# Attention over memories with a spatially gated layer behind it: new written orders for head, steady batches and last batch

## The chip, the cores and the metric

The kernel runs on one core of one Trainium2 chip. Its time is what the device takes for one execution, in microseconds (us). The kernel before took 421.38 us, the median of 3 runs (420.0 to 421.89). One more execution of it was profiled and took 421.2 us.

A core has a matrix engine (TensorE, PE in the profile), three engines for elementwise work (VectorE, DVE; ScalarE, ACT; GpSimd, POOL) and a queue that starts transfers (SyncE, SP). Each works through its own list of instructions in order and waits on semaphores for the others.

## The reference

There are 8 batches of 8 heads with 576 rows of 64 numbers. Each head compresses its keys and values into 32 memories, by weights that are a softmax over the rows; the queries attend to these. The result, 576 rows of 512 numbers, goes through a layer of two halves u and v: v is normalised per row, mixed over the rows by a 576 x 576 matrix, gates u, and is projected.

```python
a = exp(phi - max(phi, axis=rows)); a = a / (sum(a, axis=rows) + 1e-9)
k_m, v_m = einsum("bhsm,bhsd->bhmd", a, k), einsum("bhsm,bhsd->bhmd", a, v)
attn = softmax(q @ k_m.T / sqrt(64));  x = concat_heads(attn @ v_m)
h = maximum(x @ w_in, 0);  u, v = h[..., :512], h[..., 512:]
v_n = (v - mean(v)) / sqrt(var(v) + 1e-6)
out = (u * (w_spatial @ v_n + b_spatial)) @ w_out
```

w_in and w_out arrive as 64-bit floats.

## The kernel before, in words

All work is cut into threads, Python generators that emit a few instructions and stop. One token of a written list is one step of one thread. The letter names the thread, the number its slice (of rows for V and O, of channels for U and G), each quote mark one batch further ahead, and `*n` repeats it. `step` (line 796) starts or advances the thread.

- P (`memory_weights`, 290): loads phi, takes the maximum over rows, transposes it (mt, L300) and back (mb, L309), subtracts (L311), exponentiates (L318), sums (es).
- K (`memories`, 323): loads k and v, two steps of products kvm (L337) and sums, then den, two copies kmn (L364), vmn, transposes tk and tv, copies kT and vT.
- Q (`queries`, 393): loads q and brings it into shape; S (`scores`, 507): products sc (L518), four VectorE transposes (L529), maximum, subtraction, exponential, sum, and the parts ah and al of the result.
- M (`products`, 571): v_m times a half of w_in, mp (L584), rounded to a high part mh on ScalarE and a low part ml. 16 matmuls for each of M0 and M1. The prediction calls them memory products.
- V (`gate`, 598): the v half for 128 rows, pv, six matmuls (L616); V4 is the last 64 rows (L625, L626). Then relu (L621), or for V4 a copy, an addition and a relu (L635 to L637); statistics on VectorE (L640, L642); three small GpSimd steps (L645, L646, L650) that make scale and shift; normalisation on ScalarE (L655); high part vh on ScalarE (L658) and low part vl on VectorE (L660), or for V4 the tiles t1, t2 (L664 to L668).
- U (`units`, 671): the u half for 128 channels, pu (L682), two halves of six matmuls, and a ScalarE copy u (L691).
- G (`spatial`, 696): the mix over rows, ps (L720), in groups of six matmuls: the first reads V0's vh and vl, the second V1's, the third V2's, the fourth V3's and then t1 and t2. Then the gating g on VectorE (L731) and the parts gh, gl (L742, L744).
- O (`project`, 747): po (L760), two steps of six matmuls, a ScalarE copy o (L766) and a transfer out. O4 serves two batches, so it occurs in every second one, and sends two transfers (L771, L772).
- D, E, L, X, W, T, B: loading and decoding w_in and w_out (E and L one half of w_in each; L182 to L190), and preparing the spatial weights (transposes wt, L250). Z: a matmul on a constant tile (L780).

The list START emits the head: batch 0, and the parts of batches 1 and 2 that run ahead. PLAN is then gone through for batches 1 to 7. The order of tokens is the order of instructions on each engine; nothing reorders it later. Which step falls on which pass follows from a count:

```python
for at in sorted(range(len(steps)), key=lambda at: -steps[at][2]):
    key = steps[at][:2]
    upto[at] = count[key] = count.get(key, 0) + 1
...
while b + ahead < B and done.get(key, 0) < upto[at]:
    step(*key)
```

So a step that would lie past batch 7 drops out, and batch 7 goes through what is left of the same list.

The results of TensorE lie in two sets of buffers: four of one bank (tag b1: sc, mp, pv, po, kvm and all transposes) and two of two banks (tag b2: pu, ps, wt). A new tile takes a buffer that the last reader of another has left, so TensorE waits where that reader is late.

In the list before, U3's first half is preceded by V3 and V2, the memory products by U1's second half and four spatial groups after the scores, and in the last batch the copies end with O4 while O0's transfer stands behind O4's. In the head V4 and V3 are multiplied behind batch 1's scores, and on SP batch 1's k and v stand between the second and third of D0's four transfers.

Of the kernel before, what the change touches and what calls it, by code (L numbers as in the profile page):

```python
# [23 lines left out]


START = """
    Q*9 P Q P*2 K P*4 Z P*2 K P D1 P D1 P D1 P Z P Z P Q K*3 D1 P' W K D0 E0 Z K Z K E0 E1 D0 K*2 Z
    E1 K P' S E0 P' E1 S Z K K' P' B T0*2 E0 S P'*2 S*2 K' P' T0 P' S*2 T0 T2 P' S T2 E1 P' S L0 P'
    M1 T3 T2 M1 P' S M1 Z T3 S M1 S M1 T3 S T2 D0 S*2 M1 L0 M1 S P' S P' T3 D0 S*2 P' S*2 T4 S K'
    L1*2 K' L0 V2 V0 Q' K' L1 K'*2 L0 L1 K' V2 V0 T4 T1 B V2 T4*2 M0 V1 M0 Q' P'' T1 M0 X0 V0 T1 S  # L30
    M0 V0 M0 K' X0 U1 T1 V2 X1 Q' K' Q' V1 Q' M0 Q' V1 X1 K'*2 M0 V2 U3 P'' U3 U1 S' U3 P'' K'' S'
    V0 P'' U2 V2 U1 V0 P'' U0 V4 V1*2 V0 S' U0 V3 V1 V2 V4 X0 U2 S'*3 P'' V3 P'' X1 V4*2 M0' U2 U0
    M1' V3 V1 V4*2 X0 V3 X1 V4 V3 S' V3 G0 G1*3 G0 V3 X0 V4 G0 X1 X0 M0' X0 G1*2 G0 M1' G0 M0' X1 X0
    G3 M0' X1 G3 G2 M0' G1 G3 G2 X1 G0 M1' M0' P'' G0 G2 G1 M0' M1' G2 Q'' G3 P'' G0 O0 K'' P'' M1'
    G1 O3 G0 S' G2 G1 G3 G2*2 O1 G3*2 S' O3 S'*2 O3 O0 S' O0 S' P''*2 O3 O2 S' P'' O0 P''*2 S' O1
    M1' S' G2 O1 G3 O2 S' O2 M1' S' G2 O2 S' G3 O1
"""

PLAN = """
    K' V1 V4 U2 V0*2 Q' K'*2 V1*2 U0 V0 K' U2*2 V0 V3 V2 V1 U0 V3 Q' U3*2 U1 V4 V0 K' V2 V3 S' V4*2  # L40
    U3 U1 V2 S' G0*2 S'*2 V2 U1 V2*2 V3 S' G1*2 V3 V4 P'' V3 M1' S' M0' V2 M0' V4 G1 M1' S' V4 V3 S'
    M0'*2 G0 G1*2 G0 G3*2 P'' M0' G3 G0*3 G2 P'' G1 S' G0 G1 G2 P'' G0 G1 G2*2 P'' M1'*2 S' G2 G1 G3
    P'' M0' M1' O3 M1' G2 G3 M0' G2 G3*2 Q'' S' G3 O1 S' P'' Q'' M1' P'' O1 O3 G2 O2 S' O1 O3 P'' O2
    S' P'' S' P'' S' G2 S'*2 K''*2 O0 G3 S' O3 O2 O0 K'' O1 O0 V1' O2 V0' Q'' K'' Q'' V1' O4*2 P'''
    V0' K''' P''' K''' O4 V4' O4 U0' V1' P''' O0 K'' P'''
"""

ON_VECTOR = set("wtl1 wtl4 ml110 ml111 ml100 ml101 E0 E1 L0 L1 X0.sign X1.sign X0 X1".split())
# [2 lines left out]
def memory_attention_spatial_gate(  # L51
# [30 lines left out]
    B, H, S, D = q.shape  # L82
# [3 lines left out]
    P = 128  # L86
# [707 lines left out]
    threads, done = {}, {}  # L794

    def step(kind, n, b):
        key = kind, n, b
        if key not in threads:
            threads[key] = (WEIGHTS if kind in WEIGHTS else BATCH)[kind](b, n)
        done[key] = done.get(key, 0) + 1  # L800
        next(threads[key], None)

    def tokens(plan):
        for kind, n, ahead, times in re.findall(r"([A-Z])(\d?)('*)(?:\*(\d+))?", plan):
            for _ in range(int(times or 1)):
                yield kind, int(n or 0), len(ahead)

    steps = list(tokens(PLAN))  # L810
    upto, count = {}, {}
    for at in sorted(range(len(steps)), key=lambda at: -steps[at][2]):
        key = steps[at][:2]
        upto[at] = count[key] = count.get(key, 0) + 1

    E = mybir.EngineType
    with tc.manual_schedule(engines={E.PE, E.DVE, E.Activation, E.Pool, E.SP}):
        for kind, n, ahead in tokens(START):
            step(kind, n, ahead)
        for b in range(1, B):  # L820
            for at, (kind, n, ahead) in enumerate(steps):
                key = kind, n, b + ahead
                while b + ahead < B and done.get(key, 0) < upto[at]:
                    step(*key)


# [28 lines left out]
```

## Time and profile before

| | us |
|---|---|
| median of 3 runs | 421.38 |
| the profiled execution | 421.2 |
| its span, first to last instruction | 419.4 |
| TensorE busy | 400.1 (95%) |
| VectorE, ScalarE, GpSimd busy | 287.7, 231.2, 54.0 |
| first matmul | 6.32 |
| end of the last matmul's result copy | 414.71 |

Times in the views count from the span's first instruction. Matmuls are pipelined and their ends are modelled, so the distance from one start to the next tells more than a duration. A bracket behind a row gives how long its engine was idle before it, and what ended that. PEld is the loading of weights into TensorE, which runs beside the matmuls. [...]

### The profile page before, as it was taken

To read this page: it belongs to the slowest core of one execution; us is meant where nothing else is said; L and a number is where in the kernel's file an instruction comes from. 1 tells how busy PE (TensorE), PEld (TensorE's weight loads), DVE (VectorE), ACT (ScalarE), POOL (GpSimd) and SP (SyncE) were. 2 spreads that over 40 slices of the span, in tenths; PEclk is the share of its full clock that TensorE was granted. 3 is DMA by queue.
4 is the path that set the end of the run, shared out by engine and by line. 5 is a ranking of instruction groups with operands and counts; after the bars stand their busy time and mean duration, and the time that the engine had idled before them with its cause. 6 is when DMAs were issued, how large, how long until landed. Compare 5 with 4: busy or idle time off the path is not lost.

```text
span 419.4 us, 9447 instructions
## 1 busy us (share of the span) xinstructions
PE 400.1 (95%) x3965; PEld 337.8 (81%) x3965; DVE 287.7 (69%) x540; ACT 231.2 (55%) x425; POOL 54.0 (13%) x131
## 2 busy tenths in 40 slices
PE   3879998999999999999999999999999999999994
PEld 3446767989797888988798888988798888889983
DVE  1579987986978376977779476967779276844430
ACT  3569887556834376437734476337724476248321
POOL 1000233002300140003200140003200140014000
PEclk9988999999999999999999999999999999999998
DMA  8999990035941992048801991049701100020012
GB/s 295 382 368 244 290 247 37 2 112 111 175 158 58 314 120 35 0 163 260 76 2 59 324 122 18 2 163 264 71 2 76 42 13 0 2 100 2 0 52 75
DMA packets 85790, 50.70 MB, mean 121 GB/s; under 512 B 66226, under 2 KB 70322, under 8 KB 85748
## 3 DMA queue, kind: packets, MB, share of 16 engines
q1 hardware_dynamic: 85748, 50.10, 46.9%
q8 instruction: 31, 0.51, 0.5%
q14 instruction: 11, 0.09, 0.1%
HBM read 40.65 MB, written 9.44 MB: 119 GB/s over the span
## 4 chain that ended last, share of the span: by engine, by line
PE 74%; DVE 7%; ACT 6%; DMA 4%; POOL 4%; issue 2%; SPq 0%; DVEq 0%; POOLq 0%; ACTq 0%
PE ps L720 26%; PE po L760 21%; PE pu L682 7%; PE pv L616 6%; PE mp L584 4%; PE kvm L337 3%; DMA w_rem<-in_moe_w_spatial_dram 2%; PE sc L518 2%; ACT vr L655 2%; POOL sh L650 2%; DVE st L640 1%; POOL rs L646 1%; DMA q_all<-in_q_dram 1%; DMA phi_sb<-in_phi_dram 1%; DVE vr L636 1%
## 5 line engine op out<-in xcount | busy, mean ns | idle before, releaser
L720 PE MATMUL ps<-wth,vh 128*128 128x288 f32 x256 | 56.8, 303 | 1.9 <-ACT vh L658 1.5
L720 PE MATMUL ps<-wth,vl 128*128 128x288 f32 x256 | 55.0, 296 | 0.1
L720 PE MATMUL ps<-wtl,vh 128*128 128x288 f32 x256 | 54.9, 296 | 0.0
L760 PE MATMUL po<-woh,gh 128*128 128x512 f32 x128 | 51.0, 398 | 0.0
L760 PE MATMUL po<-wol,gh 128*128 128x512 f32 x128 | 50.3, 393 | 0.0
L760 PE MATMUL po<-woh,gl 128*128 128x512 f32 x128 | 50.1, 392 | 0.0
L742 ACT CAST gh<-g 128x512 fp32r<-128x512 f32 x32 | 19.1, 620 | 56.0 <-DVE g L731 56.0
L645 POOL TENSOR_SCALAR rs<-mv 128x1 f32<-128x1 f32 (+1 forms) x40 | 10.7, 267 | 286.4 <-DVE mv L642 252.2
L720 PEld LDWEIGHTS ps<-wth,vh 128*128 128x128 f32 x256 | 40.8, 188 | 8.3 <-issue 4.2
L766 ACT COPY o<-po 128x512 f32<-128x512 f32 x36 | 21.1, 586 | 47.7 <-PE po L760 46.9
L720 PEld LDWEIGHTS ps<-wth,vl 128*128 128x128 f32 x256 | 41.2, 188 | 0.5 <-DVE vl L660 0.5
L720 PEld LDWEIGHTS ps<-wtl,vh 128*128 128x128 f32 x256 | 41.3, 188 | 0.0
L731 DVE TENSOR_TENSOR g<-u,ps 128x576 f32<-128x576 f32 x32 | 24.1, 753 | 24.4 <-PE ps L720 24.4
L655 ACT ACTIVATE vr<-vr,sh,rs 128x512 f32<-128x512 f32 (+1 forms) x40 | 32.5, 812 | 10.4 <-POOL sh L650 10.4
L640 DVE BATCH_NORM_STATS2 st<-vr 128x6 f32<-128x512 f32 (+1 forms) x40 | 27.0, 674 | 10.8 <-ACT vr L621 10.8
L660 DVE TENSOR_TENSOR vl<-vr,vh 128x512 fp32r<-128x512 f32 x32 | 22.0, 687 | 17.0 <-ACT vh L658 16.7
L682 PE MATMUL pu<-ah,mh 128*128 128x288 f32 x128 | 29.3, 310 | 0.9 <-ACT u L691 0.8
L760 PEld LDWEIGHTS po<-woh,gl 128*128 128x128 f32 x128 | 24.1, 188 | 5.5
L760 PEld LDWEIGHTS po<-woh,gh 128*128 128x128 f32 x128 | 24.0, 188 | 5.0
L760 PEld LDWEIGHTS po<-wol,gh 128*128 128x128 f32 x128 | 24.1, 188 | 4.7
L682 PE MATMUL pu<-ah,ml 128*128 128x288 f32 x128 | 27.4, 296 | 0.0
L682 PE MATMUL pu<-al,mh 128*128 128x288 f32 x128 | 27.3, 294 | 0.0
(141 smaller groups left out, 853.4 us busy)
## 6 DMA issues: line engine op xcount, KB each, us to landing
kv_sb<-in_k_dram SPq DMA_DIRECT2D x8, 1152.0 KB, 7.7
kv_sb<-in_v_dram SPq DMA_DIRECT2D x8, 1152.0 KB, 9.8
out_dram<-o SPq DMA_DIRECT2D x32, 256.0 KB, 2.2
q_sb<-in_q_dram SPq DMA_DIRECT2D x28, 288.0 KB, 6.2
phi_sb<-in_phi_dram SPq DMA_DIRECT2D x8, 576.0 KB, 4.9
raw<-in_moe_w_in_dram SPq DMA_DIRECT2D x8, 512.0 KB, 11.8
raw<-in_moe_w_out_dram SPq DMA_DIRECT2D x4, 512.0 KB, 7.0
q_all<-in_q_dram SPq DMA_DIRECT2D x1, 1152.0 KB, 5.5
```

The lines of the kernel that those rows point to most:

```text
L337: nc.tensor.matmul(kvm[r][32 * j : 32 * j + 32], phi_sb[halves[r], j, i, :], kv_sb[halves[r], j, :, i * D : (i + 1) * D], start=(i == 0), ...
L584: nc.tensor.matmul(mps[r][32 * j : 32 * j + 32, :], vT[D * r : D * r + D, 32 * j : 32 * j + 32], win_sb[D * r : D * r + D, j, cs], start=True,
L616: nc.tensor.matmul(pv, x[:, r, cs], m[:, r, DM:DFF], start=(n == 0), stop=(n == 5))
L640: nc.vector.bn_stats(st6, vr)
L655: nc.scalar.activation(vr, vr, AF.Identity, bias=sh, scale=rs)
L660: nc.vector.tensor_tensor(vl[:, st, :], vr, vh[:, st, :].bitcast(F32), op=ALU.subtract)
L682: nc.tensor.matmul(pu[:, hf, 0:HALF], m[:, r, cs], a[:, r, hf * HALF : (hf + 1) * HALF], start=(n == 0), stop=(n == 5),)
L720: nc.tensor.matmul(ps[:, hf, 0:HALF], a, w[:, hf * HALF : (hf + 1) * HALF], start=(n == 0), stop=(n == len(ops) - 1),)
L731: nc.vector.tensor_tensor(g.rearrange("p (a s) -> p a s", a=2), u[:, dt, :].rearrange("p (a s) -> p a s", a=2), ps[:, :, 0:HALF], op=ALU.mult,
L742: nc.scalar.copy(hi, x)
L760: nc.tensor.matmul(po, a, w, start=(n == 0), stop=(n == 11))
L766: nc.scalar.copy(o, po)
```

## The change

The lists START and PLAN are written anew, with the same tokens in another order, and a third list, LAST, is added. PLAN now serves batches 1 to 6. Batch 7 follows LAST, in which every token is one step of that batch. The counting moves into a function `written` and is otherwise the same. No operation, tile or buffer count changes.

On the engines the places that the prediction speaks of become these. Steady batch, TensorE: ..., O2, U0 first half of the next batch, V2, U0 second half, U3 first half, tk, tv, U3 second half, V3, U1, scores, one group of G0, M1, M0, G1. ScalarE from O2's copy on: o, kmn, V1's vh, kmn, U2's copy; and after the scores: U1's copy, V4's and V2's normalisation, V4's t1, U3's copy. Head, TensorE: V3 ahead of batch 1's scores; after V4: U3, mt, U3, U0, M0, M1, two groups of G1, one of G0, one of G1, one of G0, then G1's fourth. Head, SP: all four transfers of D0, then k and v. Last batch: O2, O3, O0, O4, O1, and the transfers in that order.

```diff
 START = """
-    Q*9 P Q P*2 K P*4 Z P*2 K P D1 P D1 P D1 P Z P Z P Q K*3 D1 P' W K D0 E0 Z K Z K E0 E1 D0 K*2 Z
-    E1 K P' S E0 P' E1 S Z K K' P' B T0*2 E0 S P'*2 S*2 K' P' T0 P' S*2 T0 T2 P' S T2 E1 P' S L0 P'
-    M1 T3 T2 M1 P' S M1 Z T3 S M1 S M1 T3 S T2 D0 S*2 M1 L0 M1 S P' S P' T3 D0 S*2 P' S*2 T4 S K'
-    L1*2 K' L0 V2 V0 Q' K' L1 K'*2 L0 L1 K' V2 V0 T4 T1 B V2 T4*2 M0 V1 M0 Q' P'' T1 M0 X0 V0 T1 S
-    M0 V0 M0 K' X0 U1 T1 V2 X1 Q' K' Q' V1 Q' M0 Q' V1 X1 K'*2 M0 V2 U3 P'' U3 U1 S' U3 P'' K'' S'
-    V0 P'' U2 V2 U1 V0 P'' U0 V4 V1*2 V0 S' U0 V3 V1 V2 V4 X0 U2 S'*3 P'' V3 P'' X1 V4*2 M0' U2 U0
-    M1' V3 V1 V4*2 X0 V3 X1 V4 V3 S' V3 G0 G1*3 G0 V3 X0 V4 G0 X1 X0 M0' X0 G1*2 G0 M1' G0 M0' X1 X0
-    G3 M0' X1 G3 G2 M0' G1 G3 G2 X1 G0 M1' M0' P'' G0 G2 G1 M0' M1' G2 Q'' G3 P'' G0 O0 K'' P'' M1'
-    G1 O3 G0 S' G2 G1 G3 G2*2 O1 G3*2 S' O3 S'*2 O3 O0 S' O0 S' P''*2 O3 O2 S' P'' O0 P''*2 S' O1
-    M1' S' G2 O1 G3 O2 S' O2 M1' S' G2 O2 S' G3 O1
+    Q Z Q*3 Z P Q P*4 K Q P Q*2 P*2 K P Z P*6 K D1*2 K Z E0 K*3 D1 K Q*2 K D1 E1 E0 E1 P' Z K*2 W D0
+    P' S D0 Q S P' K Z E1 S T2 P' S E0 D0 T0 T2 Z S*3 T2 T0 S T0 D0 E0 T2 L0 E1 S*2 M1 T1 P' S T0 P'
+    S B P' M1*2 T3 L1 S K' P' M1 L0 M1 K' S*2 P'*2 S T3 S M1 T3 S Q' S Q' S P' Z L1 S M1 K' S L0 L1
+    V0 T1 P' L0 V2 V0 V2 L1 T3 T1 V0 P' V0 M0 B M0 P'*2 V0 V2 K' T1 M0*2 T4 K' P'' V0 K'*2 V0 T4 U2
+    Q' M0 K' Q' V2 V1 Q' V2 T4 X1 M0 V3 K' T4 V1 U1 V3 M0 K'*2 V1 S Q' P'' K' V3 V2 X1 U2 S' U2 P''
+    S' U1 X1 P'' V2 P'' S' V1*2 V3 U1 X1 U0 V4 V1 V4 U3 P''*2 S' U3 U0 M0' U3 S' X0 V4 X0 U0 S' M1'
+    V1 V3 G1 S' V4 X0 K'' V3 V4*2 M0' X1 P'' X0 V3 V4 M1' G1 V4 X1 G0 G1 M0'*2 G0 G1 G0 X0 S' G0 M0'
+    G1 Q'' M0' X0*2 K'' G0 X1 S' G3 X0 P''*2 G3 G0 X1 G1 G0*2 M1' G2*2 G1 M0' M1' G3 G2 G0 G3 G2 G1
+    M1' G1 O1 G2 G3 G2*3 M1' G3 P'' O0 G3 S'*2 O3 S' O3 S' O1 O3 S' O1 M1' O3 S'*4 P'' G3 O1 S' O2
+    P'' G2 G3 O2 O0 P''*2 O2 O0 O2 O0
 """
 PLAN = """
-    K' V1 V4 U2 V0*2 Q' K'*2 V1*2 U0 V0 K' U2*2 V0 V3 V2 V1 U0 V3 Q' U3*2 U1 V4 V0 K' V2 V3 S' V4*2
-    U3 U1 V2 S' G0*2 S'*2 V2 U1 V2*2 V3 S' G1*2 V3 V4 P'' V3 M1' S' M0' V2 M0' V4 G1 M1' S' V4 V3 S'
-    M0'*2 G0 G1*2 G0 G3*2 P'' M0' G3 G0*3 G2 P'' G1 S' G0 G1 G2 P'' G0 G1 G2*2 P'' M1'*2 S' G2 G1 G3
-    P'' M0' M1' O3 M1' G2 G3 M0' G2 G3*2 Q'' S' G3 O1 S' P'' Q'' M1' P'' O1 O3 G2 O2 S' O1 O3 P'' O2
-    S' P'' S' P'' S' G2 S'*2 K''*2 O0 G3 S' O3 O2 O0 K'' O1 O0 V1' O2 V0' Q'' K'' Q'' V1' O4*2 P'''
-    V0' K''' P''' K''' O4 V4' O4 U0' V1' P''' O0 K'' P'''
+    V1 K' V1 V0 U2 V4 K' U0 U3 K' V0 Q'*2 V0 V2 Q' V0 U0 K' U3 V3 Q' V2 V3*2 V2 U1 K' U1 K' U1 S'*4
+    V4 V2 V4 S' U3 V2 S' P'' V3 G0 V3*2 M1' V4 M0' G1 G0 V4 V2 P'' G1 V3 M1'*2 S' P'' G1 G0 M1' G0*2
+    Q'' G1 G3*2 S'*2 M0' G0 M0' G1 S' G3 S' M1' P'' M0' G3 S' G2 S' G1 P'' M0' G2*2 P'' G2 G1 P''
+    G0*2 M0' G0 M0' G1*2 O0 G2*2 G3 M1' G3 O3 M1' S' G2 G3 S' P'' O0 S' O3 G2 P''*2 O1 S' O0 P'' S'
+    P''*2 O1 K''*2 S' O3*2 U2' O0 V1' P''' O1 V0' Q'' G3 V1' V0' V1' O1 U2' G3 K'' V4' G2 O4 V1' O4
+    V4' O2 O4 V1' O2 K''' O2 O4 V0' K'' O2 U0' V4' P''' K''' V2'
+"""
+LAST = """
+    U2 V0*4 V1*2 V4*3 U0*2 V2*3 U3*3 V3*4 U1*3 G1*2 V2*2 V3*2 V2 V4 G0*3 V4 G1 V3 G0*2 G1*2 G0*3 G1
+    G0 G2*9 G1 G3*9 O2*4 O3*4 G1 O0*4 G1 O4*4 O1*4
 """
...
-        for b in range(1, B):
-            for at, (kind, n, ahead) in enumerate(steps):
+        for b in range(1, B - 1):
+            for (kind, n, ahead), upto in each:
                 key = kind, n, b + ahead
-                while b + ahead < B and done.get(key, 0) < upto[at]:
+                while b + ahead < B and done.get(key, 0) < upto:
                     step(*key)
+        for kind, n, _ in tokens(LAST):
+            step(kind, n, B - 1)
```

## Rows read from the trace of the kernel before

**Rows 1.** Stretches: us, busy time by engine, TensorE's granted clock, transfers' share, GB/s.
```profile
26.40:28.20 1.80, 0.07 (x2) 0.06 (x2) 0.00 (x0) 1.37 (x2) 0.00 (x0) 0.87 1.03 391
28.20:34.60 6.40, 6.40 (x30) 2.98 (x30) 5.91 (x8) 4.67 (x7) 0.00 (x0) 0.50 1.05 395
...
187.10:232.60 45.50, 45.38 (x467) 39.10 (x466) 34.43 (x67) 25.06 (x48) 6.09 (x15) 1.00 0.50 112
```

**Rows 2.** Chain that ended last, in batch 4: start us, us, what.
```profile
232.59 2.73 PE pv L616 x12
...
244.65 0.67 ACT u L691
245.36 2.65 PE pu L682 x18
248.01 1.13 PE sc L518 x32
...
250.13 3.20 PE ps L720 x24
253.33 1.88 PE mp L584 x32
```

**Rows 3.** TensorE in order of time, batch 2: start us, us, instruction.
```profile
151.12 0.39 PE L616 MATMUL pv<-mh,al 128*128 128x512 f32 x1
151.66 0.53 PE L682 MATMUL pu<-ah,mh 128*128 128x288 f32 x2 [0.16 <-ACT u L691]
```

**Rows 4.** Waits: us in total, times, longest.
```profile
ACT vr L655 <- POOL sh L650: 10.4, 13, 1.4
...
PEld pu L682 <- ACT u L691: 3.3, 6, 0.8
...
PE ps L720 <- DVE t L668: 0.2, 1, 0.2
```

**Rows 5.** TensorE in order of time, end of the head.
```profile
55.94 0.39 PE L626 MATMUL pv<-ml,ah 128*64 128x512 f32 x1
...
61.64 0.53 PE L720 MATMUL ps<-wth,vh 128*128 128x288 f32 x2 [0.37 <-ACT u L691]
...
68.21 0.54 PE L720 MATMUL ps<-wth,vh 128*128 128x288 f32 x2 [1.51 <-ACT vh L658]
```

**Rows 6.** GpSimd in order of time, head.
```profile
49.56 0.27 POOL L650 TENSOR_SCALAR sh<-mv,rs 128x1 f32<-128x1 f32 x1
...
62.01 1.50 POOL L650 TENSOR_SCALAR sh<-mv,rs 64x1 f32<-64x1 f32 x1
```

**Rows 7.** VectorE in order of time, at the same place.
```profile
62.24 2.35 DVE L184 SCALAR_TENSOR_TENSOR raw<-raw 128x1024 int32<-128x1024 int32 x2
```

**Rows 8.** TensorE in order of time, before 40 us.
```profile
28.17 0.45 PE L300 MATMUL mt<-ident,mx 128*128 128x128 f32 x1 [1.73 <-issue]
...
30.58 2.80 PE L584 MATMUL mp<-win_sb,vT 64*32 64x512 f32 x16
...
38.80 2.25 PE L337 MATMUL kvm<-kv_sb,phi_sb 64*32 64x128 f32 x144
```

**Rows 9.** SP's transfers in order of time, end: start us, us to issue.
```profile
414.73 0.47 SPq L771 DMA_DIRECT2D out_dram<-o  x1
...
415.89 0.58 SPq L769 DMA_DIRECT2D out_dram<-o  x1
```

**Rows 10.** ScalarE in order of time, batch 3.
```profile
201.92 0.65 ACT L691 ACTIVATE u<-pu 128x576 f32<-128x576 f32 x1 [1.45 <-PE pu L682]
202.47 0.81 ACT L655 ACTIVATE vr<-vr,sh,rs 128x512 f32<-128x512 f32 x1
```

**Rows 11.** SP's transfers in order of time, head.
```profile
21.71 0.38 SPq L325 DMA_DIRECT2D kv_sb<-in_v_dram  x1
25.39 1.60 SPq L173 DMA_DIRECT2D raw<-in_moe_w_in_dram  x2
```

**Rows 12.** Transfers of line 325 (k and v): issue to landing.
```profile
DMA to landing us min/median/max: 6.8/9.1/13.4
```

More of the change, by code (lines that the diff above doesn't have):

```diff
@@ L806, in tokens, with written @@
                 yield kind, int(n or 0), len(ahead)
[L810 to L814, printed above, removed]
+    def written(plan):
+        steps = list(tokens(plan))
+        upto, count = [0] * len(steps), {}
+        for at in sorted(range(len(steps)), key=lambda at: -steps[at][2]):
+            key = steps[at][:2]
+            upto[at] = count[key] = count.get(key, 0) + 1
+        return list(zip(steps, upto))
+    each = written(PLAN)
     E = mybir.EngineType
```

## The prediction

> **What bounds the kernel now.** I read the views from coarse to fine. First the table of stretches, for how full TensorE is in each stage: from about 40 us on it has no room, with 45.38 us of work in the 45.50 us that one batch takes [rows 1]. A new order of the same operations cannot shorten that work; it can remove only time in which TensorE waits, or what lies before its first and after its last matmul. Then the chain that ended last: a steady batch is gate products, unit products, scores, spatial groups and memory products end to end, with one step of ScalarE among them, the copy of a unit product [rows 2]. Then TensorE in order of time at that place: U3's first matmul comes 0.54 us after V2's last one, where matmuls of that width follow each other every 0.23 us; 0.31 us is lost [rows 3]. The waits have it six times [rows 4]. The reader is to see that this is all: a steady batch has some 0.4 us to give.
>
> The head has more. In the first spatial products of batch 0 TensorE idles 0.37, 1.51 and 0.18 us, 2.06 in all [rows 4, 5]: first for a unit copy, then for vh of V3, then for the subtraction that ends V4. Both gate slices were multiplied late (V4's last matmul at 55.94, V3's behind it), and their GpSimd steps were slow: one of 128 numbers took 1.50 us where it took 0.27 earlier [rows 6], beside 2.35 us of weight decoding on VectorE [rows 7]. [...] At the end, the last product's output is issued at 414.73 in two transfers, and O0's, finished earlier, stands behind them on SP and goes at 415.89 [rows 9].
>
> **The change part by part.** Every step occurs as often as before, the eight filler products Z among them, so nothing is added or removed; only positions on the five queues move.
>
> *The end.* In the last list O1 comes last, and its one transfer is the last on SP; O4's two lie 2.7 us of matmuls earlier. The last issue moves from 415.89 to where the first now is, 414.73: 1.16 us less [rows 9]. Ends: 0, if the landing of that transfer is slower alone, and 1.7, if the wait of the copy shrinks as well. I take 1.16.
>
> *Steady batches.* U3 must wait for U2's copy, since two unit products fill the two buffers. In the new list U0's first half, V2 and U0's second half stand between O2's last matmul and U3: 0.88 + 1.37 + 0.88 = 3.1 us, by the chain's 2.65 for three halves and 2.73 for two slices [rows 2]. In that time ScalarE must do O2's copy, two kmn, V1's vh and U2's copy, five activations of at most 0.65 (the longest, U2's copy [rows 10]), so 3.25 at most and less because two are narrow. At worst it is 0.15 late, at best not at all. Five batches from 2 to 6 give 5 x 0.35 = 1.75 (0.31 in rows 3; the six waits of rows 4, seen at the weight load, have a mean of 0.55). Ends: 0 and 2.6. What is late next: the scores, memory products and G1. G1 needs the buffer of U3, and U3's copy now stands on ScalarE behind U1's copy, two normalisations and a rounding: 0.65 + 0.81 + 0.81 + 0.65 + 0.65 = 3.57, plus 0.2 after U1's last matmul. TensorE has scores 1.13, one spatial group 0.80 and both memory products 1.88 in between, 3.81 [rows 2, 10]. It fits with 0.04 to spare if each activation ran alone; but the normalisation starts 0.55 after a copy of 0.65 began [rows 10], so some 0.4 is left. I count no new wait. The memory products follow the scores after one group (0.80), where four groups and a unit half lay between, so the banks of the scores, emptied by VectorE's transposes, are nearly due as well; the same answer.
>
> *The head, from the gate slices on.* V3 is now multiplied ahead of batch 1's scores, more than 10 us before the group that reads it, so the 1.51 goes; U0's copy and V4 remain. Between V4's product and the group that reads it lie three unit halves (2.65), two memory products (1.88) and six spatial groups (4.80): 9.3 us. In the kernel before V4 needed 13.5 us, from 56.2 to 69.65, with VectorE's decoding and V3's late subtraction ahead of its own last step. Ends of this edit: all 2.06 us gained, or 13.5 - 9.3 = 4.2 us of new wait less the 2.06 that go, a loss of 2.1. V3's subtraction, still ahead of it on VectorE, is early now, but both pieces of decoding stay ahead of it, so I take 0.36 still lost: 1.7 gained.
>
> *The head before 40 us.* On SP the last two transfers of w_in go ahead of batch 1's k and v, so v takes their slot: issued by 25.39 + 1.60 = 27.0 instead of 21.71 [rows 11], and landing 9.1 later by the median of k and v [rows 12], at 36.1. Batch 1's memories began at 38.80 [rows 8], so this costs nothing by the median; queued behind them are V0 and V2, which now follow the first half of the memories on TensorE. Against that, the second half of the first scores' softmax no longer stands behind the transpose that came 1.73 late, and runs earlier. Ends: 2.7 gained (memories at 36.1 instead of 38.80) and 1.6 lost (v lands after the longest 13.4, at 40.4). I take 0.6 gained, near the 38.80 row, since VectorE has the same work before it either way.
>
> The 1.73 us wait names no releaser [rows 8]; I keep it, on the ground that it sits beside full DMA engines and not beside a step that moved. [...] No row here decides.
>
> Sum: 1.16 + 1.75 + 1.7 + 0.6 = 5.2 off the profiled execution's 421.2 (span 419.4 and 1.8 around it), 416.0. The median of the runs, 421.38, is 0.18 above that execution: 416.2. I forecast 416.2, with 414 to 418 as its own range.
>
> **The rivals.**
> *Better: the early head shifts as a whole.* The first softmax no longer waits, the 1.73 goes or is covered, and the memories of batch 1 start when v lands by the median, 2.7 early instead of 0.6, with everything behind them. For: the scores no longer wait for that transpose. Against: VectorE's load. 416.2 - 2.1 = 414.1.
>
> *The head gives nothing.* V4 is late by what V3 no longer is. For: its cover is 9.3 against 13.5. 421.38 - 1.16 - 1.75 = 418.5.
>
> *The clock falls for longer.* [...] In the kernel before 16 memory products took 2.80 at a clock of 0.5 and 0.94 at full clock [rows 1, 2, 8], which came after 1.7 us of idling. Memories (2.2) and two slices (2.73) at half speed cost up to 4.9: 416.2 + 4.9 = 421.1, the same. [...]
>
> *Slower: ScalarE makes G1 wait in every batch.* Place: U3's copy behind two normalisations, each of which waits for GpSimd. Its reserve is 0.04 by full durations. The longest such wait was 1.4 [rows 4]; if V2's scale comes that late, G1 starts 1.36 late in batches 1 to 6, 8.2 us in all: 416.2 + 8.2 = 424.4. It decides from 1.2 late per batch, which makes 7.3. For: the queue is in order, and the normalisations stand ahead of the copy, where in the kernel before only one did. Against: V2's product ends about 7 us before, and GpSimd has by then only V2 to do.
>
> *It changes nothing.* The moved waits come back elsewhere at the same size: 421.
>
> **How the numbers follow.** Chances: forecast 0.42, better head 0.13, head nothing 0.20, clock 0.08, nothing at all 0.06, G1 slower 0.11. Two runs of this kernel are told apart from about 0.5%, 2.1 us, so faster means below 419.3 and slower above 423.5. Faster: 0.42 + 0.13 + 0.20 = 0.75. Same: 0.08 + 0.06, and 0.01 of the G1 rival, 0.15. Slower: 0.10. The range goes from 412.5, 1.6 below the better head, to 421.5, which takes in the clock and the neutral case and leaves out the G1 rival and the head's worst ends.
>
> **What would show it.** Right: one transfer issued after the last product; no wait of unit products for a unit copy from batch 2 on; TensorE's idle time before the spatial products of batch 0 below 0.6 us; batch 1's memories starting at 36 to 39. Wrong: waits of spatial or memory products in every batch (G1 rival), a stretch at clock 0.5 longer than 7 us or after 36 us (clock rival), or V4's subtraction releasing TensorE after more than 1 us (head gives nothing).

## The result: 417.0 us against 421.6, where 416.2 was forecast

Four runs of the changed kernel gave a median of 417.02 us (415.39 to 418.25), four of the kernel before 421.63; the ratio is 0.9894, with a 95% interval of 0.9848 to 0.9940. A second timing of both (below, first of the second group of experiments) gave 0.9927 (0.9900 to 0.9954), so the two timings put the gain at 0.7 and 1.1%; all thirteen executions of the changed kernel have a median of 417.86. The profiled execution took 415.39 us, its span is 413.6.

The first lines of the page of the changed kernel. Its lines of code have moved by 5 (L720 is now L725).

```profile
span 413.6 us, 9467 instructions
...
PE 397.4 (96%) x3965; PEld 336.4 (81%) x3965; DVE 284.1 (69%) x540; ACT 230.1 (56%) x425; POOL 46.6 (11%) x131
```

As many matmuls as before (3965); what changed is when they start. Five marks on TensorE have the same work ahead of them in both kernels, so that their distance can be compared: the first spatial product, the first projection product of batch 0 and of batch 6, the first matmul of the last projection product, the end of the span.

| us | before | changed | gain | forecast |
|---|---|---|---|---|
| start to the first spatial product | 61.64 | 61.63 | 0.01 | 0.6 |
| from there to batch 0's first projection | 17.54 | 15.11 | 2.43 | 1.7 |
| to batch 6's first projection | 281.72 | 280.54 | 1.18 | 1.75 |
| to the last projection product | 50.25 | 49.69 | 0.56 | 0 |
| to the end | 8.25 | 6.64 | 1.61 | 1.16 |
| sum | 419.40 | 413.62 | 5.79 | 5.2 |

The sum came out nearly as forecast, but in part from other terms. Rows of the changed kernel that answer to those of before follow. The stretches of [rows 1]: the clock is 1.00 where it had been 0.50.

```profile
26.40:28.20 1.80, 1.12 (x7) 0.65 (x7) 1.80 (x2) 1.30 (x3) 0.00 (x0) 1.00 1.01 401
28.20:34.60 6.40, 5.17 (x38) 2.87 (x38) 4.91 (x10) 6.17 (x10) 0.00 (x0) 1.00 1.04 394
```

TensorE in order of time before 40 us, for [rows 8]. Two waits for ScalarE are new, and batch 1's memories start 0.36 us earlier.

```profile
27.50 0.44 PE L255 MATMUL wt<-ident,w_sb 128*128 128x128 f32 x2 [0.68 <-issue]
...
33.10 0.50 PE L156 MATMUL mp<-mh,minus 128*128 128x512 f32 x1 [1.20 <-ACT mh L598]
...
36.71 0.53 PE L156 MATMUL wt<-wth,minus 128*128 128x256 f32 x2 [0.75 <-ACT wth L266]
...
38.44 0.84 PE L342 MATMUL kvm<-kv_sb,phi_sb 64*32 64x128 f32 x39
```

The end of the head, for [rows 5]: no bracket is left at the first spatial product, at the fourth group or at V4's tiles.

```profile
61.63 0.54 PE L725 MATMUL ps<-wth,vh 128*128 128x288 f32 x2
...
65.73 0.43 PE L725 MATMUL ps<-wth,vh 128*128 128x288 f32 x2
...
66.53 0.69 PE L725 MATMUL ps<-ws,t 128*128 128x288 f32 x4
```

U3's first matmul in batch 3, for [rows 3]: the unit product that now stands ahead of it leaves no gap.

```profile
192.03 0.42 PE L687 MATMUL pu<-ah,ml 128*128 128x288 f32 x2
192.30 0.29 PE L687 MATMUL pu<-ah,mh 128*128 128x288 f32 x1
```

The waits, for [rows 4] (engine, line, what ended the wait; us in total, times, longest). No unit product waits for a unit copy any more; instead V's products wait twice for a projection's copy, and that copy waits four times for the transfer of an earlier output.

```profile
ACT o L771 <- DMA out_dram<-o: 12.9, 4, 4.4
...
PEld pv L621 <- ACT o L771: 2.2, 2, 1.4
PE pv L621 <- ACT o L771: 1.3, 2, 0.9
```

The end, for [rows 9]: the last copy before, then the last copy and the one issue behind it in the changed kernel.

```profile
414.12 0.59 ACT L766 COPY o<-po 128x512 f32<-128x512 f32 x1 [2.18 <-PE po L760]
```

```profile
409.97 0.59 ACT L771 COPY o<-po 128x512 f32<-128x512 f32 x1 [2.17 <-PE po L765]
410.58 0.34 SPq L774 DMA_DIRECT2D out_dram<-o  x1
```

### The profile page after: what moved, and what is told of

It is laid out like the page before. It is cut to its first block, busy times and chain, and to the rows that moved or that the text cites. A ratio compares the mean times of both kernels' runs of the same rounds, so it can differ in the third digit from the quotient of the medians.

```text
span 413.6 us, 9467 instructions
## 1 busy us (share of the span) xinstructions
PE 397.4 (96%) x3965; PEld 336.4 (81%) x3965; DVE 284.1 (69%) x540; ACT 230.1 (56%) x425; POOL 46.6 (11%) x131
## 4 chain that ended last, share of the span: by engine, by line
PE 84%; DMA 5%; DVE 5%; ACT 3%; issue 1%; SPq 0%; ACTq 0%
PE ps L725 29%; PE po L765 20%; PE pu L687 12%; PE pv L621 9%; PE mp L589 3%; PE kvm L342 3%; DMA w_rem<-in_moe_w_spatial_dram 2%; DMA out_dram<-o 2%; PE sc L523 2%; DMA q_all<-in_q_dram 1%; DVE phi_sb L316 1%; PE pv L631 1%; PE pv L630 1%; PE tq L410 1%; ACT phi_sb L323 1%
## 5 line engine op out<-in xcount | busy, mean ns | idle before, releaser
L725 PE MATMUL ps<-wth,vh 128*128 128x288 f32 x256 | 57.0, 303 | 0.0
L725 PE MATMUL ps<-wth,vl 128*128 128x288 f32 x256 | 54.9, 296 | 0.0
L725 PE MATMUL ps<-wtl,vh 128*128 128x288 f32 x256 | 54.5, 294 | 0.0
L725 PEld LDWEIGHTS ps<-wth,vh 128*128 128x128 f32 x256 | 41.2, 190 | 8.7 <-ACT vh L663 5.0
L650 POOL TENSOR_SCALAR rs<-mv 128x1 f32<-128x1 f32 (+1 forms) x40 | 8.8, 221 | 328.3 <-DVE grl L749 154.0
L725 PEld LDWEIGHTS ps<-wth,vl 128*128 128x128 f32 x256 | 41.1, 188 | 0.0
L725 PEld LDWEIGHTS ps<-wtl,vh 128*128 128x128 f32 x256 | 41.0, 188 | 0.0
L626 ACT ACTIVATE vr<-pv 128x512 f32<-128x512 f32 x32 | 19.2, 600 | 19.8 <-PE pv L621 13.5
L687 PE MATMUL pu<-al,mh 128*128 128x288 f32 x128 | 27.4, 296 | 0.0
```

Source lines behind the costliest of these rows:

```text
L626: nc.scalar.activation(vr, pv, AF.Relu)
L687: nc.tensor.matmul(pu[:, hf, 0:HALF], m[:, r, cs], a[:, r, hf * HALF : (hf + 1) * HALF], start=(n == 0), stop=(n == 5),)
L725: nc.tensor.matmul(ps[:, hf, 0:HALF], a, w[:, hf * HALF : (hf + 1) * HALF], start=(n == 0), stop=(n == len(ops) - 1),)
```

## The experiments

Eleven kernels ran, in groups beside the kernel before (median 421.3, 421.4, 421.0 and 421.9 in the four groups). Ratios are to it. The marks of all profiles, as distances in us from the mark to the left:

| kernel | median, ratio (95%) | memories, batch 1 | first spatial | batch 0's projection | batch 6's projection | last product | end |
|---|---|---|---|---|---|---|---|
| before | 421.4 | 38.80 | 61.64 | 17.54 | 281.72 | 50.25 | 8.25 |
| changed | 417.02, 0.9894 (0.9848-0.9940) | 38.44 | 61.63 | 15.11 | 280.54 | 49.69 | 6.64 |
| 1 head only | 421.12, 0.9990 (0.9968-1.0012) | 39.44 | 62.60 | 15.84 | 281.42 | 50.24 | 8.23 |
| 2 batches only | 419.80, 0.9968 (0.9951-0.9986) | 38.08 | 60.82 | 17.51 | 282.57 | 49.74 | 6.64 |
| 3 third o | 416.17, 0.9880 (0.9860-0.9901) | 41.72 | 65.29 | 15.11 | 278.37 | 49.69 | 6.65 |
| 4 end back | 418.19, 0.9922 (0.9897-0.9948) | 40.20 | 63.40 | 15.84 | 280.14 | 49.73 | 8.24 |
| 5 changed, again | 417.96, 0.9927 (0.9900-0.9954) | 38.61 | 61.79 | 15.84 | 280.91 | 49.72 | 6.64 |
| 6 old to memories | 417.88, 0.9927 (0.9896-0.9958) | 39.40 | 62.94 | 15.87 | 280.33 | 49.76 | 6.65 |
| 7 and third o | 415.74, 0.9877 (0.9840-0.9914) | 39.36 | 62.89 | 17.69 | 278.55 | 49.73 | 6.64 |
| 8 more fillers | 421.22, 0.9988 (0.9961-1.0015) | 43.13 | 66.31 | 15.86 | 279.23 | 49.70 | 6.64 |
| 9 V4 statistics | 415.35, 0.9864 (0.9839-0.9889) | 41.37 | 64.70 | 15.11 | 278.27 | 49.69 | 6.65 |
| 10 fewer fillers | 418.67, 0.9931 (0.9907-0.9955) | 42.29 | 65.59 | 15.10 | 279.83 | 49.72 | 6.66 |
| 11 U3 sooner | 416.76, 0.9890 (0.9865-0.9915) | 39.89 | 63.21 | 15.11 | 280.33 | 49.69 | 6.65 |

The memories and the first spatial product are counted from the start of the span.

**1. Head only.**

```diff
 START = """
-    Q*9 P Q P*2 K P*4 Z P*2 K ...
+    Q Z Q*3 Z P Q P*4 K Q P Q*2 P*2 K ...
```

> The kernel before with the new START and its own PLAN to the end. My theory: the head ends its stalls before V3 and V4 and nothing else, so the first product of the projection starts 2.4 us earlier (76.8 instead of 79.2), the wait of U3 for U2's copy comes back five times (1.76 us together), the end keeps its 1.77 us from the last copy to the last issue: about 419.2 against 421.6. Rival, clock: what the trace shows as 2.4 us is bought by the 6.4 us at clock 0.5 that the profile of before had and that of the change had not; then the runs' median is that of before, 421.6, and runs with a lower mean clock are longer. Rival, coupling: the old PLAN meets a head that it wasn't written for and batch 1 stalls for a us or more: 420.5 or above.

Right in the second mark, wrong in the time: the stalls ahead of V3 went (15.84 against 17.54), but the first spatial product came 0.96 later, and the median gained 0.1%, which cannot be told from nothing. U3's waits and the end's 8.23 stayed. The waits of this kernel:

```profile
PE pu L682 <- ACT u L691: 1.3, 4, 0.8
```

**2. Batches only.** START of before with PLAN and LAST of the change.

```diff
 START = """
-    Q Z Q*3 Z P Q P*4 K Q P Q*2 P*2 K ...
+    Q*9 P Q P*2 K P*4 Z P*2 K ...
```

> The changed kernel with the START of before. My theory: the 2.06 us of stalls in the head are back, the rest is as in the change: no wait of U3 for U2's copy, two waits of V's products for a projection's copy (0.7 and 1.2 us), the last batch 0.5 shorter, the end 1.65 shorter; 417.0 + 2.4 = 419.4. Rival: the steady batches win only behind the new head (what the head leaves early is what hides the copies): then U3 or G1 wait again in batch 1 and 2 and the time is 420.5 or above. Rival, the head is worth nothing: 417.

419.80, 0.4 above my number. The end and the last batch kept their gain to 0.05; the stalls of the head are back (17.51). But batch 1 is longer than behind the new head, 46.80 us from projection to projection instead of 44.95, and TensorE's only wait in it, here its row, is one for the scores' part ah that the new PLAN asks for earlier than the old START makes it. Of the 1.85 us, 1.76 lie ahead of batch 2's memories, where this wait stands. So in the trace the two lists are not independent. The times, 0.1% and 0.3% apart and 0.7 or 1.1% together, point the same way, by about as much as their intervals allow for.

```profile
PE pv L621 <- ACT ah L566: 1.1, 1, 1.1
```

**3. A third buffer for o.**

```diff
-        o = two.tile([P, DM], F32, name="o")
+        o = three.tile([P, DM], F32, name="o")
```

> The changed kernel with three buffers for o, the rows of a projection's output, where it has two. In the changed kernel the third projection copy of a batch waits on ScalarE 3.9 to 4.4 us for the transfer of an earlier output to land, and TensorE's V products wait for that copy in two batches, 0.67 and 1.23 us. My theory: both waits go, 417.0 - 1.9 = 415.1, and ScalarE no longer idles before L771 for a transfer. Rival: the bank that the V product needs is then late for another reason (ScalarE does that copy right behind another, or the V relu before it), and at most 0.5 us is won: 416.5 to 417.

The theory, in the trace: the stretch between the projections is 2.17 shorter (278.37 against 280.54). Batches 3 and 6, those with the waits, give 0.67 and 1.25 of it, 1.92 together, the theory's 1.9. The other 0.25 lies in batch 2, at a stop of TensorE for which the profile names no releaser, shorter in this execution (0.18 us from one start to the next, 0.44 in the changed kernel; see the last section). In the changed kernel ScalarE stands before the third copy of a batch, and TensorE behind it, because the bank that the V product needs is the one this copy empties. ScalarE of the changed kernel, then TensorE at the same place:

```profile
182.74 0.59 ACT L771 COPY o<-po 128x512 f32<-128x512 f32 x1 [3.87 <-DMA out_dram<-o]
```

```profile
182.61 0.39 PE L621 MATMUL pv<-mh,al 128*128 128x512 f32 x1
183.38 0.50 PE L621 MATMUL pv<-mh,ah 128*128 128x512 f32 x1 [0.39 <-ACT o L771]
```

With three buffers the third copy follows the second at once (one row of two copies), and no V product waits for one. ScalarE there:

```profile
181.70 1.07 ACT L771 COPY o<-po 128x512 f32<-128x512 f32 x2
```

The median fell by 0.85 against the four runs of the first timing, and by 1.7 against the 417.86 of all thirteen. The head of this execution shows why a median of few runs hides 2 us: its first spatial product came at 65.29.

**4. The end of before.**

```diff
-    G0 G2*9 G1 G3*9 O2*4 O3*4 G1 O0*4 G1 O4*4 O1*4
+    G0 G2*9 G1 G3*9 O2*4 O3*4 G1 O1*4 G1 O0*3 O4*4 O0
```

> The changed kernel with the end of before: products O2, O3, O1, O0, O4, and O0's transfer behind O4's two. My theory: three issues stand behind the last copy instead of one, 1.77 us from the start of the last copy to the last issue where the change has 0.61, and the last transfer's landing is 0.5 longer: 417.0 + 1.65 = 418.65. Rival: only the landing of the last bytes counts, and transfers overlap so that the order of issues costs 0.3 at most: 417.3.

The theory, in the trace: 8.24 from the last product to the end, as before, 1.60 more than in the change. The median is 1.2 above the first timing of the change but only 0.3 above all thirteen executions, so the times alone do not show it. SP has the three issues of [rows 9] again:

```profile
412.70 0.47 SPq L776 DMA_DIRECT2D out_dram<-o  x1
413.22 0.59 SPq L777 DMA_DIRECT2D out_dram<-o  x1
413.86 0.58 SPq L774 DMA_DIRECT2D out_dram<-o  x1
```

**5. The change once more.** No edit.

> The changed kernel once more, unaltered, for its clock. In its profile TensorE kept clock 1.00 and the first spatial product began at 61.63; in the runs with the same START that came after, TensorE fell to 0.50 somewhere between 23 and 44 us and that product began at 62.6, 63.4 and 65.3. My theory: the profile of the change was a lucky one; over a dozen executions the mean clock lies between 0.98 and 1.00 and the time falls with it, from 415.4 at 1.00 to 418.3 at 0.983 as in the first four, so the median is 417.0 to 417.5 and this profile shows the first spatial product at 62.5 or later. Rival: the clock is an accident that costs nothing, the times do not follow it, and the first spatial product is at 61.6 again.

The times follow the clock: of the thirteen executions of the two timings, the five with a mean clock of 0.995 or more took 415.39 to 418.04 (median 416.68), the four at 0.988 or less 418.25 to 420.08 (419.5). All thirteen have a median of 417.86. My guess on the profile was wrong: it kept clock 1.00, and its first spatial product came at 61.79. So the first two marks at full clock are 61.6 to 61.8, no earlier than the 61.64 that the kernel before reached with 6.8 us at half clock.

**6. The order of before up to batch 1's memories.**

```diff
 START = """
-    Q Z Q*3 Z P Q ... L1 S M1 K' S L0 L1 V0 T1 P' L0 V2 ...
+    Q*9 P Q P*2 K ... S*2 P' S*2 T4 S K' T1 L1 Q'*2 L1 K' L0 L1 V0 T1 L0 V2 ...
```

> The changed kernel, but START follows the order of before up to the first memories of batch 1 (some 38 us), and from there the new order of what is left. My theory: the new order loses before 38 us, by three waits of TensorE for ScalarE of 2.8 us together (1.5 before a product mp, 0.4 before a transpose ta, 0.9 before a product wt), which show in all profiles with it; with the old order ahead, memories begin at 38.1 to 38.8 whatever the clock, the first spatial product at 61.3 to 62.0, the first projection 15.1 to 15.8 later, and the time is 415.5 to 416.2. Rival: what stands ahead of the memories only sets when they start, and ScalarE and VectorE, full up to 55 us, make up for any difference: 417 as the change.

My theory fell. The three waits ahead of the memories went, but these began at 39.40, the first spatial product at 62.94, and the time is that of the change. The old order up to there is not better. What follows the memories takes 22.84 and 22.74 us to the first spatial product in the two profiles with the whole old list, and 23.16 to 23.57 in the others.

**7. That with the third buffer.**

> The kernel before this in the list (START of before up to the memories of batch 1) with three buffers for o as well. My theory: the two gains add, 415.8 - 2.0 = 413.8. Rival: as the third buffer alone gave 0.85 of the runs' median, though 2.2 in the trace, they don't: 415.

The gain of the buffer is there again (278.55, and 2.1 us of the median against experiment 6), but V4 is late twice, 1.05 and 0.96 us: 17.69 to the first projection. TensorE, then GpSimd, at that place:

```profile
69.00 0.53 PE L725 MATMUL ps<-ws,t 128*128 128x288 f32 x2 [1.05 <-DVE t L673]
70.49 0.54 PE L725 MATMUL ps<-ws,t 128*128 128x288 f32 x2 [0.96 <-ACT t L671]
```

```profile
62.87 3.85 POOL L655 TENSOR_SCALAR sh<-mv,rs 64x1 f32<-64x1 f32 x1
```

**8. More fillers.**

```diff
-    ... K P Z P*6 K ...  ... P' K Z E1 S T2 ...
+    ... K P Z*4 P*6 K ...  ... P' K Z*4 E1 S T2 ...
```

> The changed kernel with six more filler products on TensorE in the head, three ahead of batch 0's memories (a wait of 1.8 us for the softmax) and three ahead of the first transposes of the spatial weights (a wait of 1.5 us for their transfer); they compute nothing that is used. My theory: the clock falls behind a stretch in which TensorE had little to do, so with these two gaps filled it stays at 1.00 in most executions, and the median is near the best of the change: 415.4 to 416. Rival, no influence: clock and times spread as in the change, median 417 to 417.5. Rival, cost: the fillers hold up what they stand before, 418.

The rival on cost, and more than it said, 421.22. The added fillers do not keep the clock (0.50 from 27.4 to 30.8). TensorE in order of time: it stops among them for 2.27 us, with no releaser named.

```profile
23.46 1.55 PE L785 MATMUL idle<-ident 128*128 128x512 f32 x3
27.29 4.00 PE L785 MATMUL idle<-ident 128*128 128x512 f32 x5 [2.27 <-issue]
```

**9. V4's statistics earlier**, on experiment 3.

```diff
-    ... M0' U3 S' X0 V4 X0 U0 ...
+    ... M0' U3 V4 S' X0*2 U0 ...
```

> The changed kernel with three buffers for o, and in START the statistics of batch 0's V4 ahead of one VectorE transpose of the scores, not behind it. In the profiles so far GpSimd's last step for V4, 64 numbers, takes 0.77 us (twice), 2.03 (five times) or 3.85 (once) with the new START, and TensorE then waits 0, 0.64 or 2.3 us for V4's tiles; it is long where it begins as VectorE starts subtractions with two inputs, and short steps of GpSimd lie beside VectorE's reductions. My theory: with the statistics some 0.4 us earlier the step fits beside the reduction, takes 0.27, the wait of 0.64 is gone in every execution, and the first projection begins 15.1 us after the first spatial product, not 15.8 or 17.7; time 415.6, where the third buffer alone had 416.2. Rival: the step's length has another cause (what VectorE runs beside it does not matter), it stays at 2.0, and the time is that of the third buffer.

The theory's numbers: the step takes 0.26, V4's wait is gone, 15.11 to the first projection, median 415.35. The three profiles with this edit (9, 10, 11) all have 0.26 and 15.10 or 15.11; of the eight with the new order here and without it, two have 15.11. This is the lowest median, 1.4% under the kernel before; the step from experiment 3 to it, 0.9880 to 0.9864, lies within the intervals. GpSimd, then VectorE beside it:

```profile
64.39 0.26 POOL L655 TENSOR_SCALAR sh<-mv,rs 64x1 f32<-64x1 f32 x1
```

```profile
63.67 1.35 DVE L540 TENSOR_REDUCE rmx<-sm 128x36 f32<-128x1152 f32 x1
64.94 0.68 DVE L665 TENSOR_TENSOR vl<-vr,vh 128x512 fp32r<-128x512 f32 x1
```

**10. Without the first six fillers**, on experiment 9: the first six `Z` of START are left out.

> The kernel before this one without the first six filler steps of START (twelve products on a constant tile, used by nothing). In all profiles so far in which TensorE ran at full clock until then, it stands still behind its 348th product, at 24.4 to 26.8 us, whatever comes next (a transpose for the softmax, one of the spatial weights, a filler), and goes on at 27.3 to 28.4. My theory: that is the next piece of the instruction stream arriving; without twelve products the 348th is twelve steps further on in the program, later than 28 us, and the stall of 0.7 to 0.9 us ahead of the third transpose of wt is gone or stands elsewhere behind the 348th. Then the time falls by up to 0.9 against the kernel before, if the clock is kept. Rival, order: the stall stays ahead of the third transpose of wt. Rival, clock: the fillers were what kept it, the fall to 0.50 comes earlier or lasts longer, and the time rises by 1 to 3 us.

The time is that of the rival on the clock, 418.67, 3.3 above experiment 9, but its cause isn't shown to be the clock alone. The mean clock of its six executions is 0.975 to 0.986, where experiment 9 had 0.987 to 0.999, and in the profile it is 0.50 over the stretch shown (columns of [rows 1]). The stall ahead of the third transpose of wt is gone, as the theory has it, but the clock was 0.50 there, and experiments 3 and 11, in which it had fallen by then too, show no such stall either; so this run doesn't tell the missing products from the clock, and it doesn't show what the stall is. Nor does any run show the gain of up to 0.9: the stall took 0.68 us in the changed kernel's profile and 1.82 in that of experiment 9. Two other things differ in this profile. The first transpose wt, which waits 2.83 us for the transfer of w_sb, begins at 28.35, in experiment 9 at 25.84. And of the 2.5 us between the two spans only 0.9 are there at the first spatial product; 1.5 come in batch 2, where TensorE stops once more with nothing named (last row).

```profile
22.80:32.50 9.70, 6.87 (x101) 5.21 (x97) 6.41 (x10) 4.56 (x6) 0.00 (x0) 0.50 1.01 366
```

```profile
137.81 0.16 PE L354 MATMUL kvm<-ones,es 64*32 64x2 f32 x1 [1.43 <-issue]
```

**11. U3 sooner**, on experiment 9.

```diff
-    V1 K' V1 V0 U2 V4 K' U0 U3 K' V0 ...
+    V1 K' V1 V0 U2 V4 K' U3 U0 K' V0 ...
```

> The kernel with three buffers for o and V4's statistics earlier (415.35), with U3's first half in PLAN ahead of U0's second half instead of behind it, so that 0.8 us less of TensorE's work covers U2's copy. In the changed kernel that copy ends 0.57 us before U3 begins (batch 3). My theory: U3 then waits again for U2's copy, 0.8 - 0.57 = 0.25 and the 0.1 to 0.2 from a copy's end to a product's start, 0.3 to 0.4 in each of the six batches, about 2 us: 417.3, and the waits of unit products for a unit copy are back in the trace six times. Rival: ScalarE adapts, as its copy waits only for U2's product, and nothing changes: 415.4.

The theory: the wait is back, seen five times, not six, and each of batches 3 to 6 is 0.38 us longer. From projection to projection it is 280.33 instead of 278.27, 2.06 us; five times 0.38 are 1.90 of it, and 0.16 is the nameless stop in batch 2. The median rose by 1.4; the ratios, taken in two groups, have intervals that overlap.

```profile
PEld pu L687 <- ACT u L696: 2.7, 5, 0.5
```

## Why the prediction was right, and where it was not

*The end: right.* From the last copy's start to the last issue it is 0.61 (410.58 - 409.97) instead of 1.77 (415.89 - 414.12), the 1.16 forecast. The other 0.45 is the landing, which I had kept as an end of the range: the span closes 3.04 behind the last issue, it was 3.51. Experiment 4 gives the sum back. The last batch gave 0.56 that I had not counted; it comes with PLAN and LAST (50.25 with the old ones, 49.7 in all others).

*U3's wait: right, and a little larger.* Taken at 1.75, it is worth 1.90 in experiment 11. The reserve was there: in batch 3 U2's copy, the row below, ended at 191.73, 0.57 before U3 began, where I had allowed it to be 0.15 late.

```profile
191.07 0.66 ACT L696 ACTIVATE u<-pu 128x576 f32<-128x576 f32 x1
```

*"I count no new wait": this step failed.* I followed the unit copies and the memory products through ScalarE's queue and left out the projection's copies, whose two output buffers come free only when a transfer has landed. The new list puts three copies close together where loads are issued too (phi and q in batch 3, by SP's rows, from 180.65 to 185.25). Outputs landed 2.0 to 5.4 us after their issue, with a median of 2.3; the third copy waits up to 4.4 us, and 1.9 us of it reach TensorE (experiment 3). Without it the steady stretch would have gained 3.10. Of that 1.9 is U3's wait as experiment 11 puts it back, 0.5 lies in batch 1, and 0.16 in the stop in batch 2, shorter in the changed kernel's profile (0.44 against 0.60). Most of the last 0.5 is U3 again: its start was 0.28 to 0.52 us late in the five batches of the kernel before, 1.75 in all, and 0.27 late in each batch of experiment 11.

*V3 and V4: right in size, with luck in the profile.* Taken at 1.7, the profile shows 2.43, experiments 1, 4, 5 and 6 show 1.67 to 1.70. The group that reads V3 never waits again with the new order; V4 costs 0, 0.7 or 2.6 us (15.11, 15.84, 17.69 to the projection), as GpSimd's last step takes 0.77, 2.03 or 3.85. One row of [rows 6] was misread: the step of 1.50 us has 64 numbers, so it is V4's last step, and V3's of 128 numbers took 0.27 (the two before it 1.1 and 1.5). What length V4's step would have in the new order was no term of the sum.

*The head before 40 us: this term failed.* I took 0.6 us gained, by memories that start earlier, and kept the wait of 1.73 us. The wait at its place was 0.68. The memories did start 0.36 earlier, at full clock; v, issued at 26.16, landed 11.8 us later, the longest of its line, and not 9.1. SP's row of it, and for [rows 12] the landings of that line:

```profile
26.16 0.38 SPq L330 DMA_DIRECT2D kv_sb<-in_v_dram  x1
```

```profile
DMA to landing us min/median/max: 6.2/8.1/11.8
```

But at the first spatial product nothing was left (from the memories on it took 23.19 us instead of 22.84), and in the eight other profiles with the new list or the end of it, and with the same fillers, it came 0.15 to 3.65 us later than before. ScalarE is the fuller engine there now, 6.17 of 6.40 us [rows 1, its column was 4.67], and holds TensorE twice. Experiment 6 shows that these two waits are not the cause by themselves. What sets this mark to the last us stays open, beyond the clock.

*The rivals.* "The head gives nothing" is what the median of experiment 1 says, for another reason than the one I gave: not V4, but what is lost ahead of it. "The clock falls for longer" holds for single executions, of both kernels: the stretch at 0.50 was 6.8 us before, none in two profiles of the change, 3.4 us in experiments 1 and 4, and two of about 7 us in experiment 3, where the first spatial product is latest. "G1 waits" did not occur: in batch 3 U3's copy ended at 200.48, and G1 began at 201.26.

*The sum.* The profiled execution is 0.6 us below the 416.0 forecast for it, the median 0.8 above 416.2, and 1.7 over all thirteen executions: the profile had full clock throughout, most executions don't. Within the sum two misses, the copies (1.9) and the head (0.6), are made up by what the steady batches (3.10 less 1.75), V4 (0.73), the last batch (0.56) and the landing (0.45) gave beyond their terms. The forecast was near by that balance as much as by its working.

## What to carry to other kernels

When operations are put in a new order, go through every pool of two buffers, not only those that the edit names: here those that a transfer empties held ScalarE up by 3.9 to 4.4 us in the two batches in which 1.9 us of it showed on TensorE. Compare two profiles by marks that have the same work ahead of them, stage by stage; sums agree by chance. And time a change of 1% over a dozen executions, when the first 40 us alone differ by 3 (batch 1's memories begin at 38.44 to 41.72 in five profiles of the same START).

## What the runs showed of the hardware

*A stall at a fixed place.* For the 1.73 us before mt [rows 8] the profile names no releaser, and the order of the steps did not decide where they stood. In the ten profiles in which the clock was 1.00 as it got there (all but 3, 10 and 11), TensorE stops behind its 348th product, whatever comes next: a transpose mt (before, experiments 2, 6, 7), one of wt (the change, 1, 4, 5, 9), a filler (8). Counted by stretches that end in the stall, here before, the change and experiment 8:

```profile
0.00:28.10 28.10, 17.69 (x348) 12.04 (x348) 12.01 (x22) 13.70 (x23) 1.85 (x10) 0.99 0.96 343
```

```profile
0.00:27.40 27.40, 18.75 (x348) 11.90 (x348) 13.42 (x24) 12.52 (x22) 1.85 (x10) 1.00 0.96 343
```

```profile
0.00:27.20 27.20, 19.92 (x348) 12.14 (x349) 12.54 (x23) 11.59 (x20) 1.85 (x10) 1.00 0.94 339
```

It goes on at 27.3 to 29.0 us, after 0.5 to 2.3. Ahead of it stand 144 short products of the scores, and the transfers' share up to there is 0.91 to 0.96 in the six profiles counted in this way (before, the change, 1, 6, 8, 9). That instructions arrive there was my theory in experiment 10. The pages of both kernels list a queue for instructions, of 31 packets and 0.51 MB, but not when its packets came, and no run shows that TensorE waited for one. A second stop with no releaser named lies in batch 2: in twelve of the thirteen profiles (all but 8) a product just behind the 1490th to 1494th starts 0.08 to 1.6 us after the one ahead of it, where its neighbours follow in 0.03 or less (0.6 before, 0.44 in the changed kernel). Experiment 10, which leaves twelve products out, still has it behind its 1493rd, as the changed kernel has, and so twelve products further on in the order. What either stop is stays open; no run took the first one away at full clock.

*A GpSimd step of several lengths.* The step of 64 numbers took 0.77, 2.03 or 3.85 us with the new order, and 0.26 in experiments 9 to 11. In experiment 5 it began as VectorE began a subtraction with two inputs, and ended with the second such subtraction; in the changed kernel it ended with the first, in experiment 7 with the fourth instruction. In all three it began 0.03 to 0.05 us ahead of the first subtraction, and the same instructions followed: which of them it outlasts is not explained by any run. GpSimd, then VectorE, of experiment 5:

```profile
61.77 2.03 POOL L655 TENSOR_SCALAR sh<-mv,rs 64x1 f32<-64x1 f32 x1
```

```profile
60.58 1.31 DVE L540 TENSOR_REDUCE rmx<-sm 128x36 f32<-128x1152 f32 x1
61.81 0.67 DVE L665 TENSOR_TENSOR vl<-vr,vh 128x512 fp32r<-128x512 f32 x1
62.41 1.34 DVE L543 TENSOR_TENSOR sm<-sm,rmx 128x1152 f32<-128x1152 f32 x1
63.68 1.21 DVE L189 SCALAR_TENSOR_TENSOR raw<-raw 128x1024 int32<-128x1024 int32 x1
```

In these three profiles the step ends within 0.13 us of the end of one of VectorE's instructions. With a start half a us further ahead of the first subtraction (0.55 in experiment 9, 0.04 in 5, though times on GpSimd are rough) it lay beside the reduction and took 0.26 instead of 2.03, 1.8 us less. That VectorE's instructions hold the step up is my reading of these rows, and no run shows it.

*The clock.* In eleven of the thirteen profiles it fell to 0.50 before 40 us, in the kernel before behind 1.80 us in which TensorE was busy for 0.07 [rows 1]. In experiments 3 and 10 it had been busy for 1.23 of 3.00 and 1.21 of 2.60 us (from 20 us on); then the clock was 0.51 over 7.00 and 0.50 over 9.70. But a second stretch of experiment 3, 0.52 over 7.00, came behind one with 5.08 of 6.30 busy, and in the changed kernel, with 1.30 of 3.50 busy (24.0 to 27.5), the clock stayed at 1.00. So three of these four falls stand behind idle time of more than half of the stretch, and how much of it brings one is not shown. Leaving six filler steps out of START cost 3.3 us of the median (experiment 10 against 9); six more cost 3.3 as well (8 against 5). Neither is a price of the clock by itself: experiment 10 also has the late w_sb and the stop in batch 2, and in experiment 8 the fillers themselves take TensorE's time (4.00 us for five products at 0.50).
